# Attention backward on one core: head groups of five instead of six, and a fourth staging tile for dV and dK

## The chip, the core and the metric

The kernel runs on one core of a Trainium2 chip. The metric is the device time of one execution in microseconds (us); the median of the runs is what counts. Beside it stands one profiled execution, from which all stretches and durations are read.

## What is computed

Two independent attention blocks, A and B, take the same shapes. Batch is 8, queries 96, model width 640, 32 heads of 128, 512 cached keys and values. All data are bfloat16.

```python
q = (x @ wq) split into heads                     # 8 x 32 x 96 x 128
p = softmax(q @ k_cache^T * 128**-0.5)            # 96 x 512 for each batch and head
o = p @ v_cache
out = (o of all heads side by side) @ wo          # 8 x 96 x 640
```

The two results are concatenated along the last axis. The kernel returns this and, for a given `grad_out`, the gradients of both blocks by x, k_cache, v_cache, wq and wo. The gradients dK and dV are as large as the caches, 33.5 MB each and block.

## The kernel before

**Ticks.** Work is laid out on a list of ticks. One tick is one batch of one head, so a head has eight ticks and the 64 heads of both blocks have 512. Each stage of one batch has an offset in ticks (`OFF`), so that in one tick the stages of several batches stand side by side; within a tick they are sorted by slot. `Emitter.run` calls them in this order, and a scheduler then makes the instruction streams of the engines, which each run in order. Where a tile has no free buffer, the scheduler puts the writing instruction behind the last reader of the old tile.

**One batch of one head.** TensorE makes the scores S (L298), VectorE the row maximum (L300), ScalarE the exponential with its row sum (L310), VectorE the reciprocal (L320), POOL the probabilities P (L329). TensorE transposes P (L365) and makes O transposed (L359). ScalarE copies both out (L375, L378). dV is four matmuls (L389), and ScalarE copies it to `dV_sb` (L392). dP (L417) and a row sum `dl` (L419) give dS on VectorE (L421). From dS come dK (L432, copied by ScalarE to `dK_sb` at L435), its transpose (L346, L348) and dQ transposed (L340).

**Staging of dV and dK.** One `dV_sb` or `dK_sb` tile holds two batches. After the second, SP issues one store of 256 KB for the pair (`c_st`, L398). Each name has three buffers (L391, L434).

**Loads.** SP also issues, in the same in-order queue, the loads of K and V (L266, two batches each) and their transposes by DMA (`KT`, `VT`, L275). The first pair of a head has its K transposed on TensorE instead (L285). POOL issues the loads of `wq_p` and `wo_h` and the stores of dwq and dwo. At the start of B, SP also loads x and grad_out for B through `ld_tmp` (L118), for TensorE to transpose (L134), and in natural layout (L144).

**Once per head.** The weights are transposed (`pB`, L210 and L216), q and dO projected (`pC`, L243), brought to natural layout (`pD`, L258), and dwo and dwq made (`qB` L470, `qD` L490).

**Group products.** The products `out = O wo` and `dx = dQ wq^T` sum over heads. They are made in groups of heads: for each of six token tiles and two column pieces (512 and 128 wide), `gU` (L512) adds the heads of a group in one PSUM bank. The first group's result is copied by ScalarE to an f32 accumulator, each further group's is added by VectorE (L516 for out, L518 for dx), and the last group's goes to the output. So each group and product has 12 such results. They are spread over ticks after the group's last head: nine ticks for out and then nine for dx if the group has HG heads, fewer in proportion for smaller groups (at least three), and nine for B's last group but one:

```python
gs0 = max(3, (GSPREAD0 * groups[g]) // HG)
...
tk = cLg + OFF["s5"] + 2 + (i * gs0) // n_out
```

**What hangs on HG.** With HG = 6 the heads of A are cut into 6, 6, 5, 5, 5, 5 (L68 to L70) and those of B into 6, 6, 6, 6, 6, 2 (L624). The number of buffers that must outlive a group follows HG: HG + 2 slots in `OD` (O and dQ transposed of a head, L661), HG + 2 buffers of `wqT_h` (L217), HG + 3 of `wo_h` (L198).

Of the kernel before, what the change touches and what calls it, by code (L numbers as in the profile page):

```python
# [11 lines left out]
BF16 = mybir.dt.bfloat16  # L12
# [41 lines left out]
def build_block(tc, em, tick0, blk, x, kc, vc, wq, wo, g_all, out_all, dx, dk, dv, dwq, dwo, ident, ones, pools, HG=6, first=True, groups=None):  # L54
# [8 lines left out]
    KC = Sk // 128  # L63
# [3 lines left out]
    HG = min(HG, H)  # L67
# [28 lines left out]
    const, ps, kvp, wk, hd, hst, grp = (pools[k] for k in ("const", "ps", "kvp", "wk", "hd", "hst", "grp"))  # L96

    def bank(shape, dt, name):
        return ps.tile(shape, dt, name=name, tag="bank")
# [3 lines left out]
    SB = {}  # L103
# [278 lines left out]
    def c_s4(h, b):  # L382
        def f():
            st = CS[(blk, h, b)]
            hs = HS[(blk, h)]
            P_sb = st["P_sb"]
            dV_ps = bank([128, KC * 128], F32, "dV_ps")
            for c in range(KC):
                nc.tensor.matmul(dV_ps[:, c * 128:(c + 1) * 128], P_sb[:, c * 128:(c + 1) * 128], hs["dOnat_h"][:, b * 128:(b + 1) * 128], start=True, stop=True)  # L389
            if b % 2 == 0:  # L390
                SB[(blk, h, b // 2, "v")] = wk.tile([128, 2, KC * 128], BF16, name="dV_sb", bufs=3)  # L391
            nc.scalar.activation(SB[(blk, h, b // 2, "v")][:, b % 2], dV_ps[:], ACT.Identity, scale=1.0)  # L392
        return f

# [30 lines left out]
    def c_s7(h, b):  # L425
        def f():
            st = CS[(blk, h, b)]
            hs = HS[(blk, h)]
            dS_sb = st["dS_sb"]
            dK_ps = bank([128, KC * 128], F32, "dK_ps")  # L430
            for c in range(KC):
                nc.tensor.matmul(dK_ps[:, c * 128:(c + 1) * 128], dS_sb[:, c * 128:(c + 1) * 128], hs["Qnat_h"][:, b * 128:(b + 1) * 128], start=True, stop=True)  # L432
            if b % 2 == 0:
                SB[(blk, h, b // 2, "k")] = wk.tile([128, 2, KC * 128], BF16, name="dK_sb", bufs=3)  # L434
            nc.scalar.activation(SB[(blk, h, b // 2, "k")][:, b % 2], dK_ps[:], ACT.Identity, scale=1.0)  # L435
        return f

# [114 lines left out]
    for g in range(NG):  # L552
        h0 = GH0[g]
        for hh in range(groups[g]):
            h = h0 + hh
# [39 lines left out]
            hk = HK if first or h < H - 1 else dict(HK, qA0=13, qB=[14, 15], qA1=16, qD=[(19, 0, 2), (19, 2, 4), (19, 4, 5)])  # L595
# [25 lines left out]


def _kernel_impl(tc, A_x, A_k_cache, A_v_cache, A_wq, A_wo, B_x, B_k_cache, B_v_cache, B_wq, B_wo, grad_out,
           out_0, out_1, out_2, out_3, out_4, out_5, out_6, out_7, out_8, out_9, out_10, HG=6, slots=None, off=None, hk=None, ev=None, gspread=None, groupsA=None, groupsB=(6, 6, 6, 6, 6, 2)):  # L624
    global GSPREAD0, GSPREAD1
    nc = tc.nc
    if slots:
        SLOTS.update(slots)
    if off:
        OFF.update(off)  # L630
    if hk:
        HK.update(hk)
    if ev:
        EV.update(ev)
    if gspread:
        GSPREAD0, GSPREAD1 = gspread
    with ExitStack() as ctx:
        P = lambda **kw: ctx.enter_context(tc.tile_pool(**kw))
        cst = P(name="gconst", bufs=1)
        ident = cst.tile([128, 128], BF16, name="ident")  # L640
        make_identity(nc, ident[:])
        ones = cst.tile([128, 1], BF16, name="ones")
        nc.vector.memset(ones[:], 1.0)
        warm = cst.tile([128, 128], BF16, name="warm")
        nc.vector.memset(warm[:], 1.0)
        pools = dict(
            const=P(name="const", bufs=1),
            ps=P(name="ps", bufs=8, space=PSUM),
            kvp=P(name="kv", bufs=11),
            wk=P(name="wk", bufs=3),  # L650
            hd=P(name="hd", bufs=2),
            hst=P(name="hst", bufs=HG + 2),
            grp=P(name="grp", bufs=1),
            stp=P(name="stp", bufs=5),
        )
        warm_ps = pools["ps"].tile([128, 128], F32, name="warm_ps", tag="bank")
        for _ in range(32):
            nc.tensor.matmul(warm_ps[:], warm[:], warm[:], start=True, stop=True)
        pools["SX"] = {}
        pools["XP"] = {}  # L660
        pools["OD"] = pools["const"].tile([128, 2, HG + 2, A_x.shape[0] * A_x.shape[1]], BF16, name="OD", bufs=1)  # L661
        pools["HS"] = {}
        pools["CS"] = {}
        em = Emitter()
        t_next = 13
        for blk, args in enumerate(((A_x, A_k_cache, A_v_cache, A_wq, A_wo, grad_out, out_0, out_1, out_2, out_3, out_4, out_5),
                                    (B_x, B_k_cache, B_v_cache, B_wq, B_wo, grad_out, out_0, out_6, out_7, out_8, out_9, out_10))):
            H_ = args[1].shape[1]
            if blk == 0:
                grps = groupsA  # L670
            else:
                grps = groupsB
            t_next = build_block(tc, em, t_next, blk, *args, ident, ones, pools, HG=HG, first=(blk == 0), groups=grps)
        for tk, (k8, k7, k5, k4) in pools["SX"].items():
            em.add(tk, SLOTS["S8"], pools["c_s8"](tk, k8, k7))
            em.add(tk, SLOTS["S5"], pools["c_s45"](tk, k8, k5, k4))
        em.run()
# [5 lines left out]
@with_exitstack  # L683
def kernel(
    ctx: ExitStack,
    tc: tile.TileContext,
    A_x: bass.AP,
    A_k_cache: bass.AP,
    A_v_cache: bass.AP,
    A_wq: bass.AP,  # L690
    A_wo: bass.AP,
    B_x: bass.AP,
    B_k_cache: bass.AP,
    B_v_cache: bass.AP,
    B_wq: bass.AP,
    B_wo: bass.AP,
    grad_out: bass.AP,
    out_0: bass.AP,
    out_1: bass.AP,
    out_2: bass.AP,  # L700
    out_3: bass.AP,
    out_4: bass.AP,
    out_5: bass.AP,
    out_6: bass.AP,
    out_7: bass.AP,
    out_8: bass.AP,
    out_9: bass.AP,
    out_10: bass.AP,
):
    _kernel_impl(tc, A_x, A_k_cache, A_v_cache, A_wq, A_wo, B_x, B_k_cache, B_v_cache, B_wq, B_wo, grad_out,  # L710
                 out_0, out_1, out_2, out_3, out_4, out_5, out_6, out_7, out_8, out_9, out_10)
# [30 lines left out]
```

## Time and profile before

| | |
|---|---|
| time, median of 3 runs (lowest to highest) | 1680.16 us (1675.77 to 1682.78) |
| the profiled execution: time | 1681.76 us |
| the profiled execution: span of its instructions | 1679.9 us |
| mean granted TensorE clock | 0.999 |
| SP and other hardware-generated transfers (q1) | 392.32 MB |
| POOL's transfers (q0) | 43.10 MB |

The profile shows for each engine the time it is busy. TensorE's matmuls are PE and its weight loads, which run beside them, PEld. VectorE is DVE, ScalarE is ACT, GpSimd is POOL, and SP is the engine that only issues transfers; SPq lines are issues. A group line has the source line, engine, operation, tiles and count, then busy time and mean nanoseconds of one, then the engine's idle time just before them and what ended it. A row of stretches has, for each engine, busy us and count, then the granted clock, the mean share in which the DMA engines were busy (transfers that overlap can bring it over 1) and what they moved. A timeline row has start, duration and instruction, and in brackets the idle time before it with what ended it.

### The profile page before, as it was taken

The page shows a single profiled execution, that of the slowest core. Times are in us where ns is not written, and L with a number is a line of the kernel's source. Part 1 is how long each engine was busy: PE and PEld are TensorE (multiplying, and loading weights), DVE is VectorE, ACT ScalarE, POOL GpSimd, SP SyncE. Part 2 cuts the span into 40 slices and gives each one's busy share as a digit, 9 for nine tenths or more (in the row PEclk, how much of TensorE's full clock was granted, in tenths as well). Part 3 has the DMA queues.
Part 4 walks back from the last instruction along what each step waited for, and adds up shares of the span by engine and source line. Part 5 has one row for each costly group of instructions (what it writes and reads, how often), then busy time and mean ns, then how long its engine had stood idle before and what let it go on. Part 6 is the DMA issues. An engine that isn't in the chain of part 4 may idle for free.

```text
span 1679.9 us, 56195 instructions
## 1 busy us (share of the span) xinstructions
PE 1648.9 (98%) x21536; PEld 1317.8 (78%) x21536; DVE 1279.4 (76%) x2930; ACT 1397.8 (83%) x3518; POOL 665.4 (40%) x1235
## 2 busy tenths in 40 slices
PE   8999999999999999999999999999999999999999
PEld 7887788778778778778777777877788778778876
DVE  6887678778778778778777766777787778778777
ACT  7998899779779879879768988997799679868974
POOL 3444344334434434434344433443344334434432
PEclk9999999999999999999999999999999999999999
DMA  9999999989999999999999999999999999999994
GB/s 264 273 295 280 247 245 283 272 225 275 251 250 261 295 239 266 295 238 273 284 244 274 285 275 253 255 265 286 226 272 289 259 241 278 286 233 255 268 266 134
DMA packets 763150, 439.02 MB, mean 261 GB/s; under 512 B 483776, under 2 KB 753472, under 8 KB 762880
## 3 DMA queue, kind: packets, MB, share of 16 engines
q1 hardware_dynamic: 750256, 392.32, 98.8%
q0 software_dynamic: 12624, 43.10, 8.6%
q8 instruction: 169, 2.77, 0.7%
q14 instruction: 101, 0.83, 0.2%
HBM read 161.09 MB, written 159.12 MB: 191 GB/s over the span
## 4 chain that ended last, share of the span: by engine, by line
PE 78%; ACT 11%; DMA 5%; issue 3%; DVE 2%; SPq 0%; POOL 0%; ACTq 0%; DVEq 0%; POOLq 0%
PE o_ps L512 12%; PE q_ps L243 11%; PE dwq_ps L490 6%; PE dK_ps L432 5%; PE dV_ps L389 5%; PE dP_ps L417 5%; PE S_ps L298 5%; DMA out_dram<-dK_sb 5%; PE dst_ps L346 4%; PE x_ps L365 4%; PE x_ps L359 4%; PE x_ps L340 4%; PE dwo_ps L470 4%; PE n_ps L258 3%; ACT dK_sb L435 2%
## 5 line engine op out<-in xcount | busy, mean ns | idle before, releaser
L329 POOL TENSOR_SCALAR P_sb<-E_sb,rinv 96x512 bf16<-96x512 bf16 x512 | 352.4, 688 | 852.8 <-DVE rinv L320 810.7
L310 ACT ACTIVATE E_sb<-S_ps,negm 96x512 bf16<-96x512 f32 x512 | 354.5, 692 | 146.3 <-DVE negm L300 144.8
L421 DVE SCALAR_TENSOR_TENSOR dS_sb<-dP_ps,dl_ps,P_sb 96x512 bf16<-96x512 f32 x512 | 381.1, 744 | 51.2 <-PE dl_ps L419 48.3
L435 ACT ACTIVATE dK_sb<-dK_ps 128x512 bf16<-128x512 f32 x512 | 306.4, 598 | 101.2 <-PE dK_ps L432 66.0
L300 DVE TENSOR_REDUCE negm<-S_ps 96x1 f32<-96x512 f32 x512 | 347.4, 679 | 46.4 <-PE S_ps L298 44.1
L392 ACT ACTIVATE dV_sb<-dV_ps 128x512 bf16<-128x512 f32 x512 | 315.8, 617 | 0.5 <-DMA out_dram<-dV_sb 0.4
L378 ACT ACTIVATE PT_sb<-x_ps 128x384 bf16<-128x384 bf16 x512 | 257.2, 502 | 0.0
L512 PEld LDWEIGHTS <-OD 128*128 128x128 bf16 x1536 | 132.1, 98 | 100.4 <-issue 1.0
L432 PE MATMUL dK_ps<-Qnat_h,dS_sb 96*128 96x128 bf16 x2048 | 198.0, 219 | 1.2 <-ACT PT_sb L378 0.8
L320 DVE RECIPROCAL rinv<-rowsum 96x1 f32<-96x1 f32 x512 | 79.8, 156 | 156.6 <-ACT E_sb L310 153.7
L389 PE MATMUL dV_ps<-dOnat_h,P_sb 96*128 96x128 bf16 x2048 | 198.2, 219 | 0.8 <-DVE dOnat_h L160 0.6
L407 POOL TENSOR_TENSOR prod<-OD,dOT_h 128x96 bf16<-128x96 bf16 x512 | 185.2, 362 | 31.3 <-ACT OD L375 29.7
L417 PE MATMUL dP_ps<-VT,dOT_h 128*96 128x512 bf16 x512 | 195.4, 382 | 0.0
L348 DVE COPY dST_sb<-dst_ps 128x384 bf16<-128x384 bf16 x512 | 177.0, 346 | 17.5 <-PE dst_ps L346 17.1
L346 PE MATMUL dst_ps<-ident,dS_sb 96*128 96x96 bf16 x2048 | 172.0, 206 | 5.3 <-ACT PT_sb L378 2.0
L340 PE MATMUL x_ps<-dST_sb,K_sb 128*128 128x96 bf16 x2048 | 170.9, 206 | 5.8 <-ACT dK_sb L435 5.1
L375 ACT ACTIVATE OD<-x_ps 128x192 bf16<-128x192 f32 (+1 forms) x515 | 171.7, 333 | 3.9 <-PE x_ps L340 3.9
L365 PE MATMUL x_ps<-ident,P_sb 96*128 96x96 bf16 x2048 | 171.9, 205 | 1.0 <-POOL P_sb L329 0.8
L359 PE MATMUL x_ps<-PT_sb,V_sb 128*128 128x96 bf16 x2048 | 172.6, 206 | 0.2 <-ACT PT_sb L378 0.2
L340 PEld LDWEIGHTS <-K_sb 128*128 128x128 bf16 x2048 | 134.1, 98 | 40.4 <-issue 7.3
L298 PE MATMUL S_ps<-KT,QT_h 128*96 128x512 bf16 x366 | 138.7, 379 | 0.4 <-ACT dK_sb L435 0.4
L243 PE MATMUL q_ps<-gT,woT_h 128*128 128x512 bf16 (+1 forms) x640 | 136.9, 325 | 1.2 <-ACT gT L157 0.6
(82 smaller groups left out, 3344.3 us busy)
## 6 DMA issues: line engine op xcount, KB each, us to landing
out_dram<-dV_sb SPq DMA_DIRECT2D x256, 256.0 KB, 4.1
out_dram<-dK_sb SPq DMA_DIRECT2D x256, 256.0 KB, 4.4
K_sb<-in_A_k_cache_dram SPq DMA_DIRECT2D x128, 256.0 KB, 4.3
V_sb<-in_A_v_cache_dram SPq DMA_DIRECT2D x128, 256.0 KB, 4.3
K_sb<-in_B_k_cache_dram SPq DMA_DIRECT2D x128, 256.0 KB, 4.2
V_sb<-in_B_v_cache_dram SPq DMA_DIRECT2D x128, 256.0 KB, 4.0
out_dram<-dwo_sb POOLq DMA_DIRECT2D x63, 160.0 KB, 3.9
out_dram<-dwq_sb POOLq DMA_DIRECT2D x31, 320.0 KB, 5.4
```

Source lines behind the costliest of these rows:

```text
L243: nc.tensor.matmul(q_ps[:], lhs(c), rhsT[:, c, t0:t0 + w], start=(c == 0), stop=(c == DC - 1))
L300: nc.vector.tensor_reduce(negm[:], S_ps[:], axis=AX.X, op=ALU.max, negate=True)
L310: nc.scalar.activation(E_sb[:], st["S_ps"][:], ACT.Exp, bias=st["negm"][:], scale=1.0, accum_out=rowsum[:])
L329: pinned(nc.gpsimd.tensor_scalar(P_sb[:], st["E_sb"][:], st["rinv"][:], 0.0, op0=ALU.mult, op1=ALU.add))
L340: nc.tensor.matmul(dQT_ps, st["K_sb"][:, c, :], st["dST_sb"][:, c * Sq:(c + 1) * Sq], start=(c == 0), stop=(c == KC - 1))
L389: nc.tensor.matmul(dV_ps[:, c * 128:(c + 1) * 128], P_sb[:, c * 128:(c + 1) * 128], hs["dOnat_h"][:, b * 128:(b + 1) * 128], start=True, s ...
L392: nc.scalar.activation(SB[(blk, h, b // 2, "v")][:, b % 2], dV_ps[:], ACT.Identity, scale=1.0)
L417: nc.tensor.matmul(dP_ps[:], hs["dOT_h"][:, tok], st["VT"], start=True, stop=True)
L421: nc.vector.scalar_tensor_tensor(dS_sb[:], dP_ps[:], dl_ps[:, 0:1], st["P_sb"][:], op0=ALU.subtract, op1=ALU.mult)
L432: nc.tensor.matmul(dK_ps[:, c * 128:(c + 1) * 128], dS_sb[:, c * 128:(c + 1) * 128], hs["Qnat_h"][:, b * 128:(b + 1) * 128], start=True, s ...
L435: nc.scalar.activation(SB[(blk, h, b // 2, "k")][:, b % 2], dK_ps[:], ACT.Identity, scale=1.0)
L512: nc.tensor.matmul(o_ps[:], src[:, t * 128:(t + 1) * 128], rhs, start=(hh == 0), stop=(hh == groups[g] - 1))
```

## The change

HG becomes 5. A's heads are then cut into 5, 5, 5, 5, 4, 4, 4 and B's into 5, 5, 5, 5, 5, 5, 2: seven groups in each block instead of six. `OD` has seven slots, `wqT_h` seven buffers and `wo_h` eight, one fewer each. `dV_sb` and `dK_sb` have four buffers each instead of three. With the shapes of the tiles, this frees 5,632 bytes in each partition and takes 4,096.

```diff
-                SB[(blk, h, b // 2, "v")] = wk.tile([128, 2, KC * 128], BF16, name="dV_sb", bufs=3)
+                SB[(blk, h, b // 2, "v")] = wk.tile([128, 2, KC * 128], BF16, name="dV_sb", bufs=4)
...
-                SB[(blk, h, b // 2, "k")] = wk.tile([128, 2, KC * 128], BF16, name="dK_sb", bufs=3)
+                SB[(blk, h, b // 2, "k")] = wk.tile([128, 2, KC * 128], BF16, name="dK_sb", bufs=4)
...
-           out_0, out_1, out_2, out_3, out_4, out_5, out_6, out_7, out_8, out_9, out_10, HG=6, slots=None, off=None, hk=None, ev=None, gspread=None, groupsA=None, groupsB=(6, 6, 6, 6, 6, 2)):
+           out_0, out_1, out_2, out_3, out_4, out_5, out_6, out_7, out_8, out_9, out_10, HG=5, slots=None, off=None, hk=None, ev=None, gspread=None, groupsA=None, groupsB=(5, 5, 5, 5, 5, 5, 2)):
```

In the built program TensorE, ScalarE, POOL and SP have as many instructions as before; VectorE has 48 more.

## Prediction

> **What bounds the kernel now.** I read the page's busy shares first, then the waits, then stretches of one head each (a head is eight ticks; one tick handles one batch; I count heads 0 to 63 over both blocks and date them by their first dK eviction), and last the timeline around one stall.
>
> ```profile
> PE 1648.9 (98%) x21536; PEld 1317.8 (78%) x21536; DVE 1279.4 (76%) x2930; ACT 1397.8 (83%) x3518; POOL 665.4 (40%) x1235
> DMA  9999999989999999999999999999999999999994
> ```
>
> TensorE is busy for all but 31.0 us of the span of 1679.9, so that is all that can be won without removing matmuls. The list of waits has one entry that looks like a shortage of buffers: ScalarE's dK eviction on stores.
>
> ```profile
> L435 ACT ACTIVATE dK_sb<-dK_ps 128x512 bf16<-128x512 f32 x512 | 306.4, 598 | 101.2 <-PE dK_ps L432 66.0 <-DMA out_dram<-dK_sb 24.1 <-PE S_ps L298 2.5
> ```
>
> Where this costs TensorE time is seen in stretches of one head: heads 9, 10, 11 have no group product, heads 12 and 13 have them, and the last row is a special place at the change of block.
>
> ```profile
> core 0: us, PE busy (x) PEld busy (x) DVE busy (x) ACT busy (x) POOL busy (x), PEclk, DMA share, GB/s
> 246.00:267.00 21.00, 20.89 (x298) 17.32 (x297) 17.14 (x40) 20.85 (x55) 10.25 (x19) 1.00 1.15 271
> 267.00:290.00 23.00, 22.96 (x319) 19.40 (x317) 18.84 (x43) 21.00 (x55) 10.28 (x19) 1.00 1.16 262
> 290.00:315.00 25.00, 23.21 (x315) 18.47 (x312) 18.08 (x42) 20.95 (x54) 10.36 (x19) 1.00 1.15 273
> 315.00:347.00 32.00, 32.00 (x388) 24.54 (x387) 23.64 (x55) 22.89 (x57) 10.15 (x19) 1.00 1.11 282
> 347.00:377.00 30.00, 29.69 (x357) 21.86 (x355) 21.82 (x50) 21.81 (x55) 10.22 (x19) 1.00 0.88 213
> 811.60:815.00 3.40, 3.40 (x31) 2.93 (x32) 1.44 (x3) 1.49 (x4) 0.66 (x2) 0.50 1.10 365
> ```
>
> In heads with products TensorE has no gap to speak of, and in the second of them the DMA share falls to 0.88. In heads without, DMA stays above 1.14, and the third of them (290 to 315) loses 1.79 us. So SP's in-order queue falls behind in the free heads and catches up in the others. From the timeline, the time from a pair's second dK eviction to the issue of its store is 3.2, 5.8, 8.8, 11.8 us at the first pair of heads 8, 9, 10, 11, then 9.0, 5.8, 4.0 at 12, 13, 14: +2.9 per free head, about -3 per head with products. The stall of head 16 shows the end of it:
>
> ```profile
> 425.58 3.70 SPq L275 DMA_TRANSPOSE KT<-K_sb  x1
> 429.38 0.53 SPq L398 DMA_DIRECT2D out_dram<-dK_sb  x1
> ...
> 436.31 0.60 ACT L435 ACTIVATE dK_sb<-dK_ps 128x512 bf16<-128x512 f32 x1 [2.75 <-DMA out_dram<-dK_sb]
> ```
>
> The store of the pair evicted at 419.7 is issued 9.7 us late, behind a transpose, and lands 6.9 us later. With three tiles its buffer is due five ticks after that eviction, 13.8 us here; 9.7 + 6.9 = 16.6 misses that by 2.75. TensorE loses 1.73 of it.
>
> **The change, part by part.** (Positions of instructions are those of the two builds.)
>
> *Matmuls.* None is added or removed. The two builds have the same TensorE instruction count, and heads that lose products pass them to other heads: 0.
>
> *Length of the free run.* Products take 18 ticks per full group. In steady B that leaves 30 free ticks of 48 (3.75 heads) before, and 22 of 40 (2.75) after; in A groups of five left 26 of 40, groups of four now leave 18 of 32. Every run loses about one head, 2.9 us of lag.
>
> *Fourth tile.* Two ticks more, 5.3 us at 2.63 a tick: the buffer is due after 19.1 us, not 13.8. But what is late next? The KT and VT transposes stand in the same SP queue. From landings, VT was ready at least 5.4 us before the matmul that reads it, and KT at worst 3.0 us before (the one issued at 935). So the lag may grow 3.0 beyond today's limit, not 5.3, before the S matmul waits for KT. I take 3.0; the ends are 0 and 5.3.
>
> *What then goes.* TensorE's gaps by head where, away from the start and the change of block, it lost over 0.4: head 5 1.27, 11 1.79, 16 1.77, 21 0.43, 33 to 37 6.48, 43 1.42, 55 0.77, 60 and 61 0.98: 14.9, less 0.08 that an undisturbed head also shows, times 13, is 13.9. All but one place was over its limit by less than 2.9, so the shorter run alone cures them. At heads 33 to 37 the excess is 6.5; less 2.9 for the head, less 3.0 for the tile, plus 1.4 because head 33 keeps fewer matmuls to catch up beside (27.1 to 25.7 us of TensorE work, columns counted in both builds): 2.0 stays. Gain **11.9**; from 8.9 (fourth tile worth nothing) to 13.9.
>
> *Change of block.* A load of `ld_tmp` issued late, at 805.03, kept TensorE waiting for 2.60 us, and the granted clock was 0.50 for the next 3.41 us (last row of the stretches), another 1.7. The products of A's last groups now lie in heads 28 and 29 instead of 27 and 28, so the free run before it is two heads instead of three: 2.9 us less lag against a wait of 2.60. Gain **4.3**; from 0 to 4.3.
>
> On the clock the Trainium skill differs ("TensorE: Matmul & The Clock Gate", What's actually happening): it lets the clock fall after an idle window of about 3.4 us. By it a wait of 2.60 would not halve the clock and the sum below would be 1668; the row shows the half clock after the shorter wait, and the row decides.
>
> *More evictions.* One more group per block and product: 2 x 2 x 12 = 48 more adds on VectorE, 24 of each width.
>
> ```profile
> L516 DVE TENSOR_TENSOR out_acc<-o_ps,out_acc 128x512 f32<-128x512 f32 x48 | 33.2, 691 | 25.8 <-PE o_ps L512 25.4
> L516 DVE TENSOR_TENSOR out_acc<-o_ps,out_acc 128x128 f32<-128x128 f32 x48 | 13.3, 278 | 0.7 <-PE o_ps L512 0.7
> ```
>
> 24 x (0.691 + 0.278) = 23.3 us of work. It lies beside matmuls: head 13 (347 to 377) has about eleven of the adds, and VectorE is busy 21.82 of 30. A group of four has its 12 adds in seven ticks, as a group of five had in A, beside a fifth fewer product matmuls. The densest such head is 25 in the new order: its VectorE durations sum to 26.1, times 0.89 for overlap (1279.4 busy over 1435 of summed durations in the whole trace) 23.2 us, against 26 of TensorE. Cost 0; uncovered, all 23.3.
>
> The rule of the Trainium skill that speaks against this stands in "TensorEngine Tiling (Array Packing)", PSUM Bottleneck: once TensorE's part shrinks, copying PSUM out may become the limit. By it the adds would be paid and the sum below would be 1690; 21.82 of 30 says there is room.
>
> *A held bank.* With HG + 2 slots, the `wqT_h` eviction of the third head after a full group waits until that group's dx products end; its PSUM bank is held (transposed at 185.1, evicted at 223.4). There are six such holds before and nine after. In the held heads (192 to 222, 347 to 377) TensorE loses 0.05 and 0.31. Cost 0, at most 3 x 0.31 = 0.9.
>
> *ScalarE in odd free heads.* It is busy 20.85 of 21.0 there. In five heads (7, 17, 39, 49, 59) the last two product ticks now fall into such an odd head. I put 0.2 us each, an estimate between 0 and 0.5: cost **1.0**.
>
> *POOL and SP* keep their instructions and order; loads of `wo_h` have one buffer fewer but stay, as before, just behind the products that free it: 0. Tail: the same two heads at the end: 0.
>
> **Sum.** 1681.76 (the profiled execution) - 11.9 - 4.3 + 1.0 = 1666.6. That execution stands 1.6 above the median of 1680.16, but its stalls are what varies, so I don't take the 1.6 off: **1667**.
>
> **Rivals.**
> *Everything goes*: nothing stays at head 33 and ScalarE hides the rest: 1681.8 - 13.9 - 4.3 = 1663.5, to 1661. For it: the order is otherwise unchanged. Against: the worst KT margin was just there.
> *Another transfer takes the place of the store*: freed of the store wait, SP lags until KT or VT is late, so that the fourth tile gives nothing, and `ld_tmp` stays late: 1681.8 - 8.9 + 1.0 = 1673.9. For it: the 3.0 us margin. Against: every place but heads 33 to 37 needs only the shorter run. There 6.5 - 2.9 + 1.4 = 5.0 would stay.
> *The transfers are the bound on average*, spreading the products only moves the waits: -4 to 0, 1678 to 1682. Against: the lag falls to 3 to 4 us in every group.
> *Slower*: VectorE becomes the bound in the product heads, thinner in matmuls but not in adds. It decides once VectorE's work per product tick passes TensorE's, which by the rows it misses by a tenth. All 23.3 exposed: 1681.8 - 16.2 + 23.3 = 1689, and up to 1705 if the stalls stay too.
>
> **How the numbers follow.** The forecast (1663.5 to 1671) 0.45; everything goes 0.16; another transfer (1671 to 1677) 0.21; no gain 0.10; slower 0.08. Half a per cent, 8.4 us, is about what a measurement of this kernel tells from no change. Faster by more (below 1671.8): 0.45 + 0.16 + 0.03 of the third = 0.64; slower (above 1688.6) 0.08; the rest 0.28. The range leaves out the last two cases: 1661 to 1678.
>
> **What would show it.** The entry "dK eviction on its store" falls from 24.1 us to under 4; TensorE's idle time from 31 to about 17; no `ld_tmp` wait and no granted clock below 1 near 811; the store's lag peaks at 9 instead of 12 except in heads 33 to 36. Wrong if S or dP waits for KT or VT, if TensorE gets gaps released by VectorE in product heads, or if ScalarE still waits for dK stores at heads 11 and 16.

## The result, and the profile after

| | before | after |
|---|---|---|
| median on one chip, 8 runs each (lowest to highest) | 1679.79 us (1675.12 to 1685.66) | 1671.02 us (1667.78 to 1672.96) |
| the profiled execution, and its span | 1681.76, 1679.9 | 1669.93, 1668.1 |

The ratio of after to before is 0.9937, with a 95% interval of 0.9912 to 0.9961: 8.8 us on the medians less, and 11.8 between the two profiled spans. 1667 had been forecast; 1671 lies in the range.

The same rows as before, first from the page:

```profile
PE 1638.2 (98%) x21355; PEld 1318.2 (79%) x21536; DVE 1303.1 (78%) x2978; ACT 1392.7 (83%) x3518; POOL 663.8 (40%) x1235
DMA  9999999999999999999999999999999999998994
```

181 matmul records are missing here (21355 of 21536), so PE's busy time can't be set against that of before, and the forecast fall of TensorE's idle time can't be read from this line. What can be read: VectorE has 23.7 us more work, the 48 adds. The groups of lines show where ScalarE's dK eviction and those adds wait:

```profile
L435 ACT ACTIVATE dK_sb<-dK_ps 128x512 bf16<-128x512 f32 x512 | 304.9, 595 | 73.6 <-PE dK_ps L432 72.6 <-PE x_ps L365 0.7
L516 DVE TENSOR_TENSOR out_acc<-o_ps,out_acc 128x512 f32<-128x512 f32 x60 | 41.4, 690 | 21.4 <-PE o_ps L512 21.2
L516 DVE TENSOR_TENSOR out_acc<-o_ps,out_acc 128x128 f32<-128x128 f32 x60 | 16.6, 277 | 0.0
```

The entry "DMA out_dram<-dK_sb 24.1" is gone from the first. Stretches of one head each, as before: head 9 is free, 10 and 11 carry the products of a group of five. The last two rows are the place at the change of block that had a half clock before, and a place at head 36.

```profile
core 0: us, PE busy (x) PEld busy (x) DVE busy (x) ACT busy (x) POOL busy (x), PEclk, DMA share, GB/s
241.00:263.00 22.00, 21.84 (x307) 17.84 (x306) 17.47 (x40) 20.96 (x55) 10.25 (x19) 1.00 1.15 276
263.00:294.00 31.00, 30.74 (x381) 24.10 (x384) 23.88 (x56) 22.50 (x57) 10.09 (x19) 1.00 1.18 274
294.00:322.00 28.00, 27.31 (x325) 20.39 (x329) 21.44 (x49) 20.83 (x53) 9.79 (x19) 1.00 1.01 252
811.60:815.00 3.40, 3.35 (x45) 2.50 (x44) 2.73 (x7) 3.40 (x10) 1.71 (x3) 1.00 1.01 315
941.80:945.20 3.40, 3.40 (x30) 2.88 (x31) 1.54 (x4) 1.69 (x5) 0.69 (x1) 0.50 0.92 295
```

The clock near 811 is 1.00 now and `ld_tmp` keeps nobody waiting. At 941.80 there is a new half clock. The timeline of SP and then of TensorE shows what stands ahead of it:

```profile
934.75 1.23 SPq L275 DMA_TRANSPOSE KT<-K_sb  x1
936.03 0.63 SPq L398 DMA_DIRECT2D out_dram<-dK_sb  x1
```

```profile
941.69 0.59 PE L298 MATMUL S_ps<-KT,QT_h 128*96 128x512 bf16 x1 [2.31 <-DMA KT<-K_sb]
```

This is what was forecast to be late next, with 2.0 us of it in the sum, though the prediction also named a wait of S for KT as a sign of being wrong. The store issued at 936.03 belongs to a pair evicted 15.3 us earlier, and with four tiles nobody waits for it; the KT transpose issued just ahead of it, at 934.75, is what the S matmul waits for, 2.31 us. The half clock that follows (3.41 us at 0.50) costs about another 1.7.

Two things in the rows of heads 9 to 11 are not as forecast. In head 10, the first with products, the DMA share does not fall (1.18): it falls only in head 11, to 1.01, against 0.88 in the second product head of before. And head 11 has 0.69 us idle though nothing is named that it waits for.

**Time lost, by stretch.** TensorE's busy share hides small gaps, as the experiments show. So I compare kernels by lost time: the time of a stretch of heads less its matmul work. That work is counted in columns in each build and taken at 512 columns in 0.213 us (2.4 columns per ns), plus a constant for each matmul that is the same for all kernels. (In the trace of before, starts of matmuls of one group lie 0.056 us apart at 128 columns and 0.215 to 0.216 at 512, which gives both.) Only differences between kernels mean something. Each row is one profiled execution: the two of the changed kernel, after and e5, agree within 0.1 at heads 5 to 29 and 38 to 61, which I call the undisturbed heads, and differ by 2.4 at heads 30 to 37.

| lost time, us | heads 5 to 29 | 30 to 37 | 38 to 61 | span |
|---|---|---|---|---|
| before | 13.2 | 16.0 | 12.9 | 1679.9 |
| after | 10.1 | 8.2 | 11.8 | 1668.1 |
| e1, groups of five, three tiles | 11.6 | 8.9 | 14.0 | 1676.1 |
| e2, groups of six, four dK tiles | 7.6 | 15.1 | 9.8 | 1670.3 |
| e3, after, small groups of A first | 9.8 | 4.8 | 11.9 | 1665.6 |
| e4, after, 80 more adds | 16.0 | 8.6 | 16.4 | 1680.5 |
| e5, after again | 10.1 | 10.6 | 11.9 | 1670.9 |
| e6, after without held banks | 5.9 | 9.2 | 6.8 | 1661.9 |
| e7, e3 and e6 together | 6.4 | 4.8 | 6.8 | 1655.6 |
| e8, e6 with groups of four | 4.2 | 3.5 | 4.4 | 1654.3 |
| e9, e6 with seven banks | 21.9 | 18.3 | 22.7 | 1704.2 |
| e10, e4 without held banks | 10.6 | 12.1 | 9.1 | 1671.2 |
| e11, before with shorter holds | 18.1 | 18.0 | 8.4 | 1687.6 |

After gains 7.8 at heads 30 to 37, where 8.4 was forecast (4.1 of the stalls, 4.3 at the change of block). In the undisturbed heads it gains 4.3 (13.2 + 12.9 - 10.1 - 11.8, from unrounded values), where 6.8 was forecast.

### The profile page after: what moved, and what is told of

Same layout as the page of the kernel before. It is cut to its first block, busy times and chain, and to the rows that moved or that the text cites. A ratio compares the mean times of both kernels' runs of the same rounds, so it can differ in the third digit from the quotient of the medians.

```text
span 1668.1 us, 56047 instructions
## 1 busy us (share of the span) xinstructions
PE 1638.2 (98%) x21355; PEld 1318.2 (79%) x21536; DVE 1303.1 (78%) x2978; ACT 1392.7 (83%) x3518; POOL 663.8 (40%) x1235
## 4 chain that ended last, share of the span: by engine, by line
PE 81%; ACT 10%; issue 4%; DVE 3%; DMA 1%; POOL 0%; SPq 0%; ACTq 0%; DVEq 0%; POOLq 0%
PE q_ps L243 12%; PE o_ps L512 11%; PE dwq_ps L490 6%; PE dK_ps L432 6%; PE dV_ps L389 6%; PE dP_ps L417 5%; PE S_ps L298 5%; PE dst_ps L346 5%; PE dwo_ps L470 4%; PE x_ps L365 4%; PE x_ps L359 4%; PE x_ps L340 4%; PE n_ps L258 3%; PE nat_ps L455 2%; ACT E_sb L310 2%
## 5 line engine op out<-in xcount | busy, mean ns | idle before, releaser
L512 PEld LDWEIGHTS <-OD 128*128 128x128 bf16 x1536 | 135.7, 98 | 103.2 <-issue 1.3
L389 PE MATMUL dV_ps<-dOnat_h,P_sb 96*128 96x128 bf16 x2048 | 198.2, 219 | 1.3 <-DVE dOnat_h L160 0.6
L365 PE MATMUL x_ps<-ident,P_sb 96*128 96x96 bf16 x2048 | 171.9, 205 | 1.6 <-POOL P_sb L329 1.3
L512 PE MATMUL o_ps<-wo_h,OD 128*128 128x128 bf16 (+1 forms) x705 | 134.0, 292 | 3.3
```

The costliest lines, as they stand in the source:

```text
L512: nc.tensor.matmul(o_ps[:], src[:, t * 128:(t + 1) * 128], rhs, start=(hh == 0), stop=(hh == groups[g] - 1))
```

## The experiments

The experiments ran on three chips, one for each of e1 to e4, e5 to e8 and e9 to e11. There the kernel before took 1685.69, 1686.48 and 1682.89 us, so ratios, not times, are to be set against the result above.

**e1: the groups without the tiles.** My theory was that the shorter free run alone cures all stalls but those at heads 33 to 37; the rival, that the tile does it. The changed kernel with

```diff
-... name="dV_sb", bufs=4)
+... name="dV_sb", bufs=3)
-... name="dK_sb", bufs=4)
+... name="dK_sb", bufs=3)
```

> Groups of five with three dV and dK tiles, so the free runs are one head shorter but a dK buffer is due after 13.8 us as before. My theory (lag of SP's queue against the time a buffer is due): the dK waits at heads 5, 11, 16, 43, 55 and 60 are gone, since the lag peaks at 9 to 12 us there; the wait for ld_tmp and the half clock at 811 are gone; only heads 33 to 37 still wait for dK stores, 5.0 us of TensorE idle by the prediction's sum (in place of the 2.3 us wait for KT and the 1.7 us of half clock that the changed kernel has). Time 1670 to 1674, ratio to before 0.994 to 0.997. Rival (the fourth tile is what pays): the dK waits stay near 24 us in total, and the time stays at 1677 to 1682.

Measured: 1679.72 us (12 runs, 1673.04 to 1690.37), ratio to before 0.9971 (0.9951 to 0.9992). Its dK eviction still waits for stores:

```profile
L435 ACT ACTIVATE dK_sb<-dK_ps 128x512 bf16<-128x512 f32 x512 | 305.0, 596 | 86.5 <-PE dK_ps L432 68.6 <-DMA out_dram<-dK_sb 16.1 <-PE x_ps L365 0.7
```

16.1 of 24.1 us are still there, in 15 waits. The places at heads 5, 11, 16 and 43 are free, as expected, but besides heads 34 to 36 there are waits at heads 4, 14 and 15, 19 and 20, 61 and 62. The `ld_tmp` wait is gone, as forecast, which makes most of the 7 us gained at heads 30 to 37. The step "the shorter run alone cures them" falls. The lags in the trace of after suggest why: at the first pair of heads 8 to 12 they are 8.9, 10.2, 11.9, 5.2, 5.3 us. A head with products is lighter in a group of five, so SP catches up only to 5, not to 3, and the next run starts from there: the peak is 12, not 9. That lighter heads are the reason is argued, not tested.

**e2: the tile without the groups.** The kernel before, with the loads' staging (`ld_tmp`) one buffer smaller to make room:

```diff
-... name="dK_sb", bufs=3)
+... name="dK_sb", bufs=4)
-            stp=P(name="stp", bufs=5),
+            stp=P(name="stp", bufs=4),
```

> The kernel before with a fourth dK tile alone (the staging pool for ld_tmp has four buffers instead of five, to make room). My theory: the lag still climbs to 12 us and over in the free runs of three and more heads, but a buffer is due only after 19.1 us, so dK waits fall from 24.1 us to under 3; what is late next is KT, at heads 33 to 37, where 6.5 - 3.0 = 3.5 us of TensorE idle stay as a wait for KT, with up to 1.7 us of half clock behind it; the ld_tmp wait of 2.6 us and its half clock stay, since the free run before it is still three heads. Time 1671 to 1676, ratio 0.994 to 0.998. Rival (the transfers are the bound on average): the waits only move to KT and VT, over 10 us of TensorE idle on them, 1678 to 1682. Second rival (the shorter free run is what pays): as before within 2 us.

Measured: 1670.95 us (6 runs, 1667.86 to 1677.82), ratio 0.9926 (0.99 to 0.9952). One edit thus gives as much as the whole change (0.9937, and 0.9917 when run again in e5). No dK eviction waits for a store any more; the late one is the other store, dV, which still has three tiles:

```profile
L392 ACT ACTIVATE dV_sb<-dV_ps 128x512 bf16<-128x512 f32 x512 | 314.7, 615 | 13.0 <-DMA out_dram<-dV_sb 9.2 <-PE dst_ps L346 1.7 <-PE o_ps L512 1.0
```

I had expected KT to be late next, by 3.5 us; it was not at all; the dV waits, 9.2 us in ten, came first. `ld_tmp`, which has one buffer fewer here, stays late (3.2 us in 4 waits, with a half clock of 3.41 us after one of 2.20). So by the table the tile gains 8.7 in the undisturbed heads, and going on to groups of five (e2 to after) costs 4.4 there (from unrounded values).

**e3: is the rest at head 36 the free run there?** The three groups of four of A put first, so that the run at heads 30 to 37 changes:

```diff
-... groupsA=None, ...
+... groupsA=(4, 4, 4, 5, 5, 5, 5), ...
```

> The changed kernel with block A cut into 4, 4, 4, 5, 5, 5, 5 instead of 5, 5, 5, 5, 4, 4, 4: A's last group then has five heads, so its products last to head 34 and 3.9 us more of matmuls lie beside the loads of x and grad_out in natural layout that B issues in head 33. My theory: the lag at head 36 falls by about 3 us, the wait of 2.31 us for KT there and the half clock behind it (1.7 us) go, and nothing else changes: 4 us less than the changed kernel, 1666 to 1668. Rival (what keeps the changed kernel above the forecast lies elsewhere, for instance in the product heads): the wait may go but the time stays within 1 us of the changed kernel, 1670 to 1672.

Measured: 1667.33 us (6 runs, 1666.25 to 1669.81), ratio 0.9906 (0.9881 to 0.993). The KT wait and its half clock are gone, and only heads 30 to 37 change (8.2 to 4.8). The KT wait thus hung on what lies beside that run.

**e4: do the 48 adds cost?** The dearest suspect for the 4.4 us. 80 more adds on VectorE: in the middle groups two of the six token tiles are added a second time, into a tile that nobody reads.

```diff
+                if 0 < g < NG - 1 and t in (0, 3):
+                    junk = wk.tile([128, 512], BF16, name="junk", bufs=1)
+                    nc.vector.tensor_tensor(junk[:, 0:w], o_ps[:], acc[:, t, c0:c0 + w], op=ALU.add)
```

> The changed kernel with 80 more adds on VectorE: in every group but the first and the last of a block, the adds of token tiles 0 and 3 are also written to a tile that nobody reads (same operands in PSUM and in the accumulator, bf16 result). That is 40 x 0.69 + 40 x 0.28 = 38.8 us more work on VectorE in the product heads, 1.7 times what the change added. My theory (the added adds lie beside matmuls): the time stays within 3 us of the changed kernel, 1669 to 1674. Rival (VectorE is the bound in product heads): most of the 38.8 us is paid, 1690 and over; if half of it, 1690.

Measured: 1684.25 us (12 runs, 1680.1 to 1685.75), ratio 0.9992 (0.9976 to 1.0007): of the 38.8 us added (40 x 0.691 + 40 x 0.278) some 9 to 13 are paid: 13 between the medians of e4 and after, which were not run side by side, 9 by their ratios to before, 12.4 and 9.6 against the spans of after and e5. Both theories miss. The second add reads the same PSUM tile as the first, so it keeps a bank longer, too: this pointed at the banks.

**e5 and e6: the held bank.** e5 is the changed kernel once more. e6 gives `wqT_h` two buffers more, so that its eviction, in the third head after a group, no longer waits for the dx products with its PSUM bank held:

```diff
-            wqT_h = hst.tile([128, D], BF16, name="wqT_h")
+            wqT_h = hst.tile([128, D], BF16, name="wqT_h", bufs=HG + 4)
```

> The changed kernel once more, unedited, so that the next three are compared with it on the same chip. Both theories: 1668 to 1673.

> The changed kernel with two more buffers for wqT_h (nine instead of seven), so that its eviction no longer waits for the end of a group's dx products and no PSUM bank is held for some 38 us. The prediction put these holds at 0 (0.9 at most). My theory now: they are the added cost that the prediction missed, since TensorE loses about 1 us in each group of five in the ticks after the hold begins and nothing of the kind in groups of four, which have no hold. The loss at heads 6, 11, 16, 17, 21, 38, 43, 48, 53, 58 goes, 7 us in all: 1662 to 1666. Rival (VectorE's 48 more adds are the added cost): the gaps stay where they are, within 1 us of the changed kernel.

Measured: e5 1671.13 us (6 runs, 1668.51 to 1675.5), ratio 0.9917 (0.9896 to 0.9938); e6 1663.21 us (4 runs, 1661.52 to 1664.43), ratio 0.9868 (0.9844 to 0.9891). The held banks cost 7.9 us on the medians, 9.3 in the undisturbed heads of the two profiles. In e5's trace the wait for KT is longer than in that of after, the same kernel:

```profile
944.37 0.42 PE L298 MATMUL S_ps<-KT,QT_h 128*96 128x512 bf16 x1 [4.22 <-DMA KT<-K_sb]
```

One tick in the second product head, 43, shows how a held bank costs time. In after the tile is held from 1114.8 to 1151.9 us, and from 1143.4 on the next head's as well. First TensorE in after, with the bank held:

```profile
1131.30 0.34 PE L365 MATMUL x_ps<-ident,P_sb 96*128 96x96 bf16 x4
1131.72 0.40 PE L389 MATMUL dV_ps<-dOnat_h,P_sb 96*128 96x128 bf16 x4
1131.99 0.38 PE L417 MATMUL dP_ps<-VT,dOT_h 128*96 128x512 bf16 x1
1132.20 0.16 PE L419 MATMUL dl_ps<-ones,prod 128*96 128x1 bf16 x1
1132.47 0.49 PE L455 MATMUL nat_ps<-ident,OD 128*128 128x128 bf16 x6
```

The same tick in e6:

```profile
1129.11 0.34 PE L365 MATMUL x_ps<-ident,P_sb 96*128 96x96 bf16 x4
1129.28 0.39 PE L389 MATMUL dV_ps<-dOnat_h,P_sb 96*128 96x128 bf16 x4
1129.55 0.42 PE L417 MATMUL dP_ps<-VT,dOT_h 128*96 128x512 bf16 x1
1129.82 0.16 PE L419 MATMUL dl_ps<-ones,prod 128*96 128x1 bf16 x1
1129.84 0.49 PE L455 MATMUL nat_ps<-ident,OD 128*128 128x128 bf16 x6
```

Read the starts, not the durations. From L365 to L389 it is 0.42 us in after and 0.17 in e6; from L419 to L455 0.27 and 0.02. Both matmuls that come late open a new PSUM tile. Yet neither row of after has a bracket with idle time: the modelled end of a matmul reaches past the start of the next (0.17 apart, 0.34 long), so a gap of a quarter of a microsecond leaves hardly a trace in the busy column.

**e7: both.** e3's order of groups and e6's buffers.

> Both edits in the changed kernel: block A cut into 4, 4, 4, 5, 5, 5, 5 and nine buffers of wqT_h. If the two losses are separate (KT's lateness at head 36 with its half clock, 3.4 us; the held bank, 7 us), they add up: 1658 to 1662. Rival (adds): as with the new cut alone, 1666 to 1668.

Measured: 1657.22 us (4 runs, 1656.11 to 1657.41), ratio 0.9831 (0.9808 to 0.9855). That is 13.9 us less than e5, where the two alone gave 7.9 and 3.7 (e3 against after, not run side by side): they add up, and a little more. e6 still had two waits for KT (1.50 and 1.82 us); e7 has none.

**e8: still more adds, no held bank.** Groups of four throughout, which brings 72 more adds on VectorE than after has:

```diff
-... HG=5, ..., groupsB=(5, 5, 5, 5, 5, 5, 2)
+... HG=4, ..., groupsB=(4, 4, 4, 4, 4, 4, 4, 2, 2)
```

> HG = 4 with no held bank: A in eight groups of four, B in 4, 4, 4, 4, 4, 4, 4, 2, 2, and HG + 4 buffers of wqT_h: another 72 adds on VectorE (24 x 1 in A, 24 x 2 in B), 35 us by their rows, and still shorter free runs. Beside the nine buffers with groups of five: if adds beside matmuls are free once no bank is held, within 2 us of it; if adds are paid at the quarter that the 80 extra adds showed (10.5 of 38.8 us in undisturbed heads), 7 to 9 us slower than it.

Measured: 1656.71 us (5 runs, 1655.75 to 1662.07), ratio 0.9838 (0.9812 to 0.9863). It is 6.5 us faster than e6, and by the table it loses less in the undisturbed heads, too (8.6 against 12.7). Its free runs are shorter, which is part of that. With HG = 4 a group again spreads its 12 results over nine ticks; so further adds with PSUM tiles of their own are hidden if they come no denser than that. Denser ones were not tried.

The PSUM Bottleneck section of the Trainium skill's page "TensorEngine Tiling (Array Packing)", weighed in the prediction, warns that copying PSUM out may become the bottleneck after a fourfold speedup of TensorE; no run here has such a speedup, and e8's adds are not seen to be paid.

**e9: what is a bank worth?** e6 with

```diff
-            ps=P(name="ps", bufs=8, space=PSUM),
+            ps=P(name="ps", bufs=7, space=PSUM),
```

> The kernel with nine wqT_h buffers, with seven PSUM banks in the pool instead of eight: no eviction is held up, but TensorE always has the one bank fewer that it had during a hold. My theory (what the hold costs is the bank): the gaps of the changed kernel come back in the product heads and spread to ticks that had no hold, so at least the 8 us of the hold: 1671 or more. Rival (the cost comes from the late eviction itself, its place on VectorE or the weights' late readiness, not from the bank): within 2 us of 1663.

Measured: 1702.7 us (6 runs, 1698.52 to 1705.94), ratio 1.011 (1.0079 to 1.014): 39.5 us more than e6 (on another chip; 40.7 by the ratios), and in the table some 0.65 per head of the undisturbed stretches ((21.9 + 22.7 - 5.9 - 6.8) / 49), in free heads too. It also shows that the bank is what a hold costs. By the measure of the table, with 0.0035 us for each matmul, the three ticks of head 43 that lose most in after, those from 1130.9, 1135.3 and 1141.8 us, lose 0.51, 0.31 and 0.24 us; the same ticks lose 0.53, 0.31 and 0.25 in e9, which holds no tile but has one bank fewer, and 0.20, 0.00 and 0.00 in e6. Its page:

```profile
PE 1670.5 (98%) x21536; PEld 1325.0 (78%) x21536; DVE 1322.9 (78%) x2978; ACT 1400.8 (82%) x3518; POOL 664.2 (39%) x1235
```

This line and that of before have all 21536 matmuls. e9's span is 24.3 us longer (1704.2 against 1679.9), and 21.6 of it are booked as busy (1670.5 against 1648.9): the busy column counted the waits as work. It is 98% in both.

**e10: e4 again without held banks.** If e4's cost came from the held bank, they should nearly go; if VectorE is short, they should stay. (dV_sb has three buffers here, to make room.)

> The 80 extra adds (38.8 us by their rows) put into the kernel with nine wqT_h buffers; dV has three tiles again, to make room for the tile that the extra adds write. With a bank held they cost 13 us. My theory: they cost mainly because an add done twice keeps its PSUM bank longer when banks are short; with all eight banks in turn they cost under 4 us beside 1663.2, 1663 to 1667. Rival (VectorE's time as such): the same 13 us, 1675 or more.

Measured: 1672.6 us (11 runs, 1670.13 to 1676.97), ratio 0.9935 (0.9916 to 0.9953). In the undisturbed heads the 80 adds cost 6.9 us beside e6, where they cost 10.5 beside after; dV waits (6.5 us of ScalarE's idle time in six places) are little of the 6.9, since four of the six places, with 5.6 us, lie at heads 34 to 36. Both theories miss: a third went with the held banks, the rest stays. These adds double the time that a product's bank is kept, and VectorE's work too; which of the two is paid was not told apart.

**e11: the held banks of the kernel before.** If groups of six pay for held banks as well, before should gain about 4 us from

```diff
-            wqT_h = hst.tile([128, D], BF16, name="wqT_h")
+            wqT_h = hst.tile([128, D], BF16, name="wqT_h", bufs=HG + 3)
```

> The kernel before with one more buffer of wqT_h (nine instead of eight): each of its six holds of some 38 us becomes one of 10 us, at the end of a group's dx products. Store waits stay as they are. My theory: of the loss of about 1 us per full group that the kernel before shows in its second product head, half a microsecond to one goes, 3 to 6 us in all, ratio 0.996 to 0.998; the waits for dK stores may grow by part of it, since TensorE then gives SP's queue less time to catch up. Rival (the hold cost nothing before, as the prediction read it): ratio 1.000 within 0.002.

Measured: 1684.19 us (12 runs, 1672.69 to 1691.32), ratio 0.9988 (0.996 to 1.0017): no gain that can be told. The six holds of 38 us are six of 8.7 now. The lost time of the second product heads did fall, from 0.99 to 0.13 us each (heads 13, 45, 51, 57). But the stores' waits grew:

```profile
L435 ACT ACTIVATE dK_sb<-dK_ps 128x512 bf16<-128x512 f32 x512 | 306.5, 599 | 105.9 <-PE dK_ps L432 70.0 <-DMA out_dram<-dK_sb 30.3 <-PE wqT_ps L216 1.1
```

30.3 us in 23 waits, against 24.1. A reading that would fit is that with three tiles the stores set the pace: what TensorE wins in a product head is time in which SP would have caught up, and it is given back in the next free run. The trace does not show this. Heads 38 to 61 keep their gain (12.9 to 8.4). The loss grows at heads 5 to 29 and 30 to 37, but also by 5.2 us at head 4, ahead of the first tile that was held (185.1 us), where the edit can't act. This execution is the second slowest of the twelve, and its granted clock was 0.50 in four stretches, 17.1 us in all, which cost about 8.5; before has one such stretch, of 3.41 us (the last microseconds of both left out):

```profile
122.50:125.90 3.40, 3.40 (x25) 2.66 (x23) 2.67 (x6) 1.02 (x3) 1.02 (x2) 0.50 0.54 144
313.70:317.00 3.30, 3.30 (x22) 2.17 (x20) 1.70 (x4) 3.10 (x9) 1.02 (x2) 0.50 1.19 329
822.30:829.00 6.70, 5.16 (x40) 4.06 (x41) 2.27 (x6) 4.03 (x10) 1.35 (x3) 0.50 1.19 307
921.30:924.60 3.30, 3.30 (x24) 2.54 (x23) 2.57 (x6) 2.10 (x5) 1.02 (x2) 0.50 1.66 227
```

Each goes with a wait of TensorE, behind a dK store at three places and for `ld_tmp` at 822. Why the median did not fall stays open.

## Why the prediction was right, and where it was off

*Fourth tile and dK stores.* Right in what goes: 24.1 us of waits to none. Right in what is late next, and where: KT at heads 33 to 37, 2.31 us against 2.0. That the sizes agree is luck: in e5's trace of the same kernel the wait is 4.22. The half clock after that wait (0.50 for 3.41 us, about 1.7) was left out of the sum, though the prediction read the same at the change of block.

*Length of the free run.* "The shorter run alone cures them" was wrong (e1), and so was the weight put on it. The fourth dK tile alone is enough: 8.7 in the undisturbed heads (e2). The shorter run alone gains 0.5 there (13.2 + 12.9 - 11.6 - 14.0), or some 5 if the 4.8 that its additional held banks cost (below) are put back, and leaves 16.1 us of waits. The lag peaks at 10 to 12 us, not at 9. The sum survived because the two steps were taken together, and what they were forecast to give in the undisturbed heads, 7.8, is near what the tile alone gives. That is luck.

*Change of block.* Right: the `ld_tmp` wait and its half clock are gone, and e1 shows that the groups did it. The margin is small: a wait for `ld_tmp` of 1.19 us is back in e6, without a half clock.

*More evictions.* Cost 0 was right for the adds as they are, as far as e8 shows: it has more of them and is faster. e4 and e10 show that there is a limit: adds of a second pass on the same bank cost 0.27 and 0.18 us per us in the undisturbed heads (10.5 and 6.9 of 38.8).

*A held bank.* **This step failed.** "Cost 0, at most 3 x 0.31 = 0.9": nine holds cost 9.3 us (e5 to e6). Before paid already: 0.5 at each of heads 7 and 39, and 0.87 at each of 13, 45, 51, 57 (0.99 less the 0.13 that e11 leaves), about 4.5. The difference, 4.8, is what groups of five cost in the undisturbed heads (4.4, e2 to after). The error lay in the reading: idle time of 0.05 and 0.31 was taken for the loss, and that column hides such gaps.

*ScalarE in odd free heads.* 1.0 was forecast. Of the five heads three (7, 39, 49) lost at most 0.1 more than the other odd free heads; heads 17 and 59 lost about 0.8 and 0.3 more, in e6 too. That this makes 1.1 in all is luck; no experiment says what it is.

Summed: 8.7 + 7.8 - 4.4 = 12.1 by the table, 11.8 between the profiled spans, 15.2 forecast. The 4.8 of the additional held banks, forecast as 0, are more than the whole miss of 3.4.

## What to carry to other kernels

Where several tiles hang on one in-order queue, ask for each what its margin is: take the stores' wait away and the next thing on that queue is late (dV in e2, KT in after). A PSUM tile whose eviction waits for something far off is one bank fewer for everybody while it lasts, and the way to see its price is the distance between the starts of matmuls against their columns, not the busy share. Mending the banks alone gave nothing that can be told where the stores had three tiles (e11), and 7.9 us where they had four (e6); e7 and e8, at 1657 us, mend the queue and the banks and beat both kernels.

## What was not expected of the hardware

The granted clock fell to 0.50 for 3.41 us after TensorE waits of 2.20 us (e2), 2.31 (after) and 2.60 (before), in after and before about 0.1 us after the wait's end, in e2 1.4 us after it. The length of the wait alone does not decide: in e11 the clock fell after waits of 1.64, 1.69 and 1.70 us, and in e4 it stayed at 1.00 after one of 1.95. In e11 the four falls began at 122.49, 313.63, 822.22 and 921.21 us, which lie 56, 149 and 29 times 3.4133 us apart. So in that execution they lie on one grid; that it matters where on it a wait lies is a guess that no run tested.

The Trainium skill ("TensorE: Matmul & The Clock Gate", What's actually happening) has the clock fall after an idle window of about 3.4 us; the waits listed here were shorter, and the rows decide.

One PSUM bank of eight is worth 39.5 us of 1663 (2.4%) here, in a kernel whose TensorE is listed as 98% busy either way. The figure sets e9 against e6, on two chips.
